# Attention and two expert stages in one kernel: undivided attention rows with their sums, keys' subtractions shared by VectorE and GpSimd, v copies on GpSimd, slots' rows scaled by GpSimd, later x stores

## The chip, the cores and the metric

The kernel runs on one core of one Trainium2 chip. The metric is the time of one execution in device microseconds. The kernel before took 1201.28 us, the median of three runs (1198.95 to 1202.61). The engines carry their names in the profile: PE is TensorE, PEld its weight loads, DVE is VectorE, ACT is ScalarE, POOL is GpSimd, SP is SyncE, which issues most DMAs.

## The reference, cut to what matters

Three stages are chained. The first is an attention without a score matrix, over 8 batches, 8 heads, 576 positions and 64 dimensions; then each of the 4608 tokens goes to the one expert of eight that its gate logits choose; then a product of two linear maps follows, with two more linear maps behind it.

```python
q_s = exp(q - max(q, axis=-1)); q_s = q_s / (sum(q_s, axis=-1) + 1e-9)
k_s = exp(k - max(k, axis=2));  k_s = k_s / (sum(k_s, axis=2) + 1e-9)
x   = einsum('bhsd,bhde->bhse', q_s, einsum('bhsd,bhse->bhde', k_s, v))   # to (4608, 512)
logits = x @ w_gate + modality_bias[modality_id]
e_idx  = argmax(logits, axis=1); gate_w = softmax(logits)[e_idx]
out[e_idx == e] = gate_w * (relu(x @ w1[e]) @ w2[e])                      # 512 -> 1024 -> 512
y = (((out @ m1) * (out @ m2)) @ w3) @ w_out
```

## The kernel before, in words

**Order of the work.** The function body() hands every step to a planner, the class Plan: a step has an engine, a guessed cost, the function that issues its instructions, and keys that it reads and writes. Plan.order() goes through the steps by readiness and priority, and the instructions are then emitted in that order; each engine runs its own in order. SP's DMAs stand in one queue, in the same way.

**Attention.** The batches are taken two at a time, in four chunks c = 0 to 3, with two sets of buffers (z = c % 2). load() brings k, q and v of a chunk, each by two DMAs of 1152 KB. keys(c) takes the maximum over positions on DVE (L304 to L307), transposes it on PE, reduces it (L316) and spreads it back to rows (L321, and ACT's copy kr, L324). Then k - kr is formed in 12 pieces of 128x384 (L330: on DVE for c = 0, on GpSimd for c = 1 to 3) and ACT takes the exponential (L331). kvs(c) copies v beside a column of ones (vp, ACT, L342), multiplies keys by values on PE (L349), divides by the keys' sums on DVE (L356 to L358, which write bd), and multiplies the result by the gate weights (L362 to L373), so that each head's 64 columns of bd are followed by one column of ones and eight columns of gate logits: 73 in all. queries(n) subtracts the row maximum of q for three of the nine token groups of a chunk (L384, L385). attend(c, j) transposes a group (PE, L399), takes the exponential (ACT, L402) and multiplies by bd (PE, L412). The 65th column of its result is the sum of a query row's exponentials, so the result must be divided by it: ACT copies the sum with 1e-9 added (L422) and the logits (L423), DVE takes the reciprocal (L424) and multiplies 512 columns by it on the way from PSUM to xt (L425). Two groups at a time are stored to x_dram (L429).

**Routing.** route(c) turns logits into the expert, the gate weight and the place of each token. early_table() and early_lists() make, from chunks 0 and 1 alone, a table of the first three slots (tab) and the lists of their tokens (ordt, written at L621 and L622), by comparing places with block numbers (L604 to L609) and one product on PE (L614).

**Slots.** A slot is up to 512 tokens of one expert. slot(P, n) loads the expert's w1 (L706) and w2, gathers the tokens' rows of x_dram by indirect DMA from POOL's queue (L715), scales each row by its gate weight (ACT, L719), transposes it (PE, L735), splits it in a high and a low part (ACT L739, DVE L740), does the same with the weights (L686 on ACT; L688 on DVE, two of eight on GpSimd) and multiplies (PE, L760, L782). All of the slots' big buffers lie where the attention's lay, so the first split waits for the last step of the attention (the key "Mb"). In the first slots GpSimd also scatters the order of all tokens (L436), and DVE and GpSimd turn the last stage's weights from 64-bit to 32-bit numbers (doubles(), L807 to L815).

**Last stage.** Products by Strassen's scheme follow (L1113, L1246). The change does not touch them.

## Time and profile before

| | |
|---|---|
| median of three runs | 1201.28 us |
| the profiled execution | 1204.72 us |
| its span | 1203.0 us |
| PE busy | 1127.9 us, 94% of the span |
| DVE busy | 855.5 us, 71% |
| ACT busy | 525.6 us, 44% |
| POOL busy | 534.8 us, 44% |
| mean granted clock of TensorE | 0.977 |

The span is that of one execution, from the first to the last instruction; the time has 1.7 us around it. The shares are averages over stages with different limits, so a stretch has to be read by itself. PE's row of the page's second part shows 3 6 7 7 7 9 9 8 in tenths over the first eight slices of 30 us, and 9 in all behind them but the last, which has 6.

### The profile page before, as it was taken

How to read it: one execution, taken by the hardware profiler on the slowest of the kernel's cores; microseconds unless marked ns; L12 is line 12 of the kernel's file. 1: busy time of each engine (PE TensorE's matmuls, PEld its weight loads, DVE VectorE, ACT ScalarE, POOL GpSimd, SP SyncE). 2: the span in 40 equal slices, each digit the busy share in tenths (PEclk: the TensorE clock that was granted, in tenths of full speed). 3: DMA queues.
4: the chain of work that ended last, by engine and by line, in shares of the span. 5: the costliest groups of instructions: out<-in, count | busy, mean ns of one | idle time of the engine just before them, and what ended most of it. 6: DMA issues, size and time to landing. Idle time of an engine off the chain costs nothing.

```text
span 1203.0 us, 22890 instructions
## 1 busy us (share of the span) xinstructions
PE 1127.9 (94%) x8605; PEld 1025.8 (85%) x8605; DVE 855.5 (71%) x1441; ACT 525.6 (44%) x1003; POOL 534.8 (44%) x538
## 2 busy tenths in 40 slices
PE   3677799899999999999999999999999999999996
PEld 3566677788788888888988999999999999999995
DVE  7989887897688887877566666657575679765550
ACT  3555465334344544533555242423232445655550
POOL 0444148663253333242241555455555576343332
PEclk9978899999999999999999999999999999999998
DMA  9982577555275467373753343434343429987741
GB/s 352 389 331 82 178 193 182 135 201 202 92 253 163 124 214 206 102 247 137 252 182 127 99 139 104 133 118 120 118 125 117 142 88 282 345 250 232 235 143 46
DMA packets 156140, 216.01 MB, mean 180 GB/s; under 512 B 19790, under 2 KB 90994, under 8 KB 156018
## 3 DMA queue, kind: packets, MB, share of 16 engines
q1 hardware_dynamic: 148946, 195.00, 50.3%
q0 software_dynamic: 7072, 19.44, 5.5%
q8 instruction: 69, 1.13, 0.4%
q14 instruction: 53, 0.43, 0.1%
HBM read 156.35 MB, written 74.82 MB: 192 GB/s over the span
## 4 chain that ended last, share of the span: by engine, by line
PE 68%; DMA 2%; DVE 0%; issue 0%; SPq 0%; ACT 0%; POOL 0%; POOLq 0%; ACTq 0%; DVEq 0%
PE pb L1113 29%; PE pb L1246 13%; PE pb L782 11%; PE pb L760 9%; PE pb L1004 4%; DMA ca<-w_f 1%; PE pb L735 1%; DMA p_dram<-ca 1%; PE pb L991 1%; DMA ca<-p_dram 0%; DVE ar L978 0%; SPq L970 0%; POOL out_dram L1220 0%; SPq L1209 0%; DVE ca L1089 0%
## 5 line engine op out<-in xcount | busy, mean ns | idle before, releaser
L1113 PE MATMUL pb<-al,ar 128*128 128x384 f32 x1728 | 308.5, 336 | 1.1 <-ACT sx L1119 0.8
L1113 PEld LDWEIGHTS pb<-al,ar 128*128 128x128 f32 x1728 | 301.1, 188 | 1.6 <-ACT sx L1119 1.1
L782 PE MATMUL pb<-ar 128*128 128x512 f32 (+1 forms) x960 | 214.0, 381 | 0.0
L760 PE MATMUL pb<-ar 128*128 128x512 f32 (+1 forms) x960 | 213.4, 383 | 0.0
L760 PEld LDWEIGHTS pb<-ar 128*128 128x128 f32 x960 | 174.7, 190 | 34.3 <-DVE ar L747 0.3
L782 PEld LDWEIGHTS pb<-ar 128*128 128x128 f32 x960 | 172.8, 188 | 32.8
L1246 PE MATMUL pb<-ar 128*128 128x256 f32 x1512 | 182.9, 283 | 2.8 <-ACT ar L977 1.6
L1246 PEld LDWEIGHTS pb<-ar 128*128 128x128 f32 x1512 | 181.8, 192 | 3.8 <-ACT ar L977 1.8
L978 DVE TENSOR_TENSOR ar<-ca,ar 128x512 fp32r<-128x512 f32 x140 | 107.8, 779 | 54.3 <-ACT ar L977 50.7
L977 ACT CAST ar<-ca 128x512 fp32r<-128x512 f32 x140 | 86.1, 622 | 45.1 <-DMA ca<-p_dram 15.0
L746 ACT ACTIVATE ar<-pb 128x512 fp32r<-128x512 f32 (+1 forms) x80 | 46.0, 577 | 116.3 <-PE pb L760 104.0
L812 POOL TENSOR_TENSOR ca<-ca 128x512 f32<-128x512 f32 x40 | 56.7, 1422 | 78.1 <-DVE ca L811 73.4
L1119 ACT COPY sx<-pb 128x384 f32<-128x384 f32 x96 | 46.0, 481 | 90.5 <-PE pb L1113 63.9
L747 DVE SCALAR_TENSOR_TENSOR ar<-pb,ar 128x512 fp32r<-128x512 f32 (+1 forms) x80 | 52.6, 659 | 39.1 <-ACT ar L746 37.9
L330 POOL TENSOR_TENSOR kt<-kt,kr 128x384 f32<-128x384 f32 x36 | 44.1, 1263 | 73.8 <-ACT kr L324 57.6
L1147 POOL TENSOR_TENSOR ca<-ca 128x384 f32<-128x384 f32 x48 | 53.5, 1115 | 49.3 <-DVE ca L1147 49.3
L785 ACT COPY yo<-pb 128x512 f32<-128x512 f32 (+1 forms) x40 | 22.6, 566 | 107.7 <-PE pb L782 94.5
L1122 POOL TENSOR_TENSOR ca<-ca,sx 128x384 f32<-128x384 f32 x24 | 27.7, 1156 | 83.2 <-ACT sx L1119 83.2
L688 DVE TENSOR_TENSOR ar<-w2r,ar 128x512 fp32r<-128x512 f32 x60 | 44.9, 775 | 27.3 <-ACT ar L686 25.2
L1119 ACT COPY ca<-pb 128x384 f32<-128x384 f32 x48 | 23.0, 481 | 87.2 <-PE pb L1113 87.2
L1113 PE MATMUL pb<-thm,ar 128*128 128x384 f32 x288 | 59.0, 340 | 0.0
L715 POOL DMA_INDIRECT ca<-x_dram,ord x38 | 38.3, 1008 | 45.5 <-DVE ord L622 20.6
(286 smaller groups left out, 1757.8 us busy)
## 6 DMA issues: line engine op xcount, KB each, us to landing
p_dram<-ca SPq DMA_DIRECT2D x168, 192.0 KB
ca<-p_dram SPq DMA_DIRECT2D x126, 256.0 KB
w1r<-in_moe_w_dram SPq DMA_DIRECT2D x10, 2048.0 KB
w2r<-in_moe_w_dram SPq DMA_DIRECT2D x10, 2048.0 KB
ca<-in_moe_w_dram SPq DMA_DIRECT2D x32, 512.0 KB
kt<-in_k_dram SPq DMA_DIRECT2D x8, 1152.0 KB
qt<-in_q_dram SPq DMA_DIRECT2D x8, 1152.0 KB
vt<-in_v_dram SPq DMA_DIRECT2D x8, 1152.0 KB
```

The source lines that it names most:

```text
L746: P.add("S", ps_(N), lambda hh=hh, p=p: SC.activation(hh(), p(), AF.Relu), r=[K("bk", pb), "Mb"], w=[K("hh", h, m) for h in hs])
L747: P.add("V", vt_(N), lambda hh=hh, hl=hl, p=p: V.scalar_tensor_tensor(out=hl(), in0=p(), scalar=0.0, in1=hh().bitcast(F32), op0=ALU.max, o ...
L760: PE.matmul(p(), lhsT=W1(i)[:, TURN[kk], ms], rhs=XT(z)[:, kk, cols], start=(kk == 0 and c == 0), stop=(kk == 3 and c == 2))
L782: PE.matmul(p(), lhsT=W2(i)[:, f, ns], rhs=HT(y)[:, f, cols], start=(f == 0 and c == 0), stop=(f == 7 and c == 2))
L812: P.add("G", gt_(512), lambda: G.tensor_tensor(Tf, Tf, Qf, op=ALU.add), r=[K("Q", b)], w=[K("T", b)])
L977: P.add("S", (ps_ if psum else sb_)(n), lambda: SC.copy(hi(), src), r=sk, w=[hk], pri=pri)
L978: P.add("V", vt_(n), lambda: V.tensor_tensor(lo(), src, hi().bitcast(F32), op=ALU.subtract), r=list(sk) + [hk], w=[lk], pri=pri)
L1004: PE.matmul(bank[pb], lhsT=th(i, quarter_of(fb, z), g, 1)[:, 0], rhs=WO(y, 4 * z + g), start=(z == 0 and g == 0 and n == 0), stop=(z == 1 ...
L1113: PE.matmul(bk(j), lhsT=Mt[:, f, a, i, m, t], rhs=X(y, x)[:, t], start=(fresh and t == 0 and n == 0), stop=(t == 1 and n == 2), skip_group ...
L1119: P.add("S", ps_(HB), lambda j=j, to=to: SC.copy(S(to), bk(j)), r=[bkk(j)], w=[sk(to)])
L1147: P.add(eng, c(HB), lambda: e.tensor_tensor(t[:, sl], x, y, op=op), r=kk, w=[k_])
L1246: PE.matmul(bk(j), lhsT=At[z][:, m, i, f], rhs=Bt[:, x, y, f], start=(fresh and f == 0 and n == 0), stop=(f == 3 and n == 2), skip_group_c ...
```

## The change

- **x rows undivided, with their sums.** attend() no longer divides. ACT copies the sum with the eight logits (72 columns) and then the 512 columns with each head's sum as a 65th (520 columns) to xt. Rows of x_dram are 520 wide (XW). The division comes later: route() adds 1e-9, takes the reciprocal and multiplies the logits; a slot does the same with its gathered rows.
- **Keys.** For c = 1 to 3 the 12 subtractions alternate between DVE and GpSimd; for c = 0 all stay on DVE.
- **v copies.** All 16 go from ACT to GpSimd.
- **Slots' rows.** In slot 0 DVE does the division and the gate weight in one instruction per tile. In the other slots DVE makes the factors (8 per row) and GpSimd multiplies 512 columns by them.
- **x stores.** Those of chunk 3 are issued after the gathers of slot 0 have landed.
- **Tables.** early_table() is written anew with fewer instructions, its constants are made at the start, and what only main_table() needs of it moves there. In early_lists() the block numbers and their products stand ahead of the comparisons of L604. The staging buffers of doubles() are named anew over the same columns.

```diff
 def keys(c):
         for g in range(4):
             hs = slice(2 * g, 2 * g + 2)
             kg = [K("k", z, g)]
-            en, e_, c_ = ("G", G, gt_(1152)) if c else ("V", V, vt_(1152))
-            for js in (slice(3 * i, 3 * i + 3) for i in range(3)):
+            for i in range(3):
+                en, e_, c_ = ("G", G, gt_(1152)) if c and "VG"[(3 * g + i) % 2] == "G" else ("V", V, vt_(1152))
+                js = slice(3 * i, 3 * i + 3)
                 P.add(en, c_ / 3 + 0.05, lambda hs=hs, e_=e_, js=js: e_.tensor_tensor(k_[:, hs, js], ..., op=ALU.subtract), r=[K("kr", z)], w=kg)
 def kvs(c):
-            P.add("S", sb_(1152), lambda g=g, w_=w_: SC.copy(w_[:, :, :, 0:64], v_[:, 2 * g : 2 * g + 2]), ...)
+            en, e_, c_ = ("G", G.tensor_copy, 1.5) if ('GGGG', 'GGGG', 'GGGG', 'GGGG')[c][g] == "G" else ("S", SC.copy, sb_(1152))
+            P.add(en, c_, lambda g=g, w_=w_, e_=e_: e_(w_[:, :, :, 0:64], v_[:, 2 * g : 2 * g + 2]), ...)
 def attend(c, j):
-        P.add("S", 0.22, lambda: SC.activation(by_bank(r_.unsqueeze(2)), pv[:, :, :, 64:65], AF.Identity, bias=eps), r=pk, w=[qk])
-        P.add("S", 0.22, lambda: SC.copy(by_bank(l_), pv[:, :, :, 65:73]), r=pk, w=[lk])
-        P.add("V", 0.2, lambda: V.reciprocal(r_, r_), w=[qk])
-        P.add("V", vt_(512), lambda: V.tensor_tensor(xdst, pv[:, :, :, 0:64], by_bank(r_.unsqueeze(2)).to_broadcast([128, 2, 4, 64]), op=ALU.mult), r=pk + [qk, lk], w=[rkey])
+        l_, lk = l2[z][:, j].rearrange("p e (b h) -> p b h e", b=2), K("l2", z, j)
+        P.add("S", 0.28, lambda: SC.copy(l_, pv[:, :, :, 64:73]), r=pk, w=[lk])
+        P.add("S", ps_(XW), lambda: SC.copy(xdst, pv[:, :, :, 0:65]), r=pk, w=[rkey])
...
+            if c == B // 2 - 1:
+                kept.append(store)
+            else:
+                store()
 def route(c, after=()):
-        vv(lambda: V.tensor_tensor(l2_, l2_, rq_.unsqueeze(3).to_broadcast([128, H, NT, E]), op=ALU.mult), ...)
+        vv(lambda: V.tensor_scalar(l2_[:, :, 0], l2_[:, :, 0], 1e-9, None, op0=ALU.add), r=list(after), w=l2k)
+        vv(lambda: V.reciprocal(l2_[:, :, 0], l2_[:, :, 0]), w=l2k)
+        vv(lambda: V.tensor_tensor(l2_[:, :, 1:], l2_[:, :, 1:], l2_[:, :, 0:1].to_broadcast([128, NT, E, H]), op=ALU.mult), ...)
 def slot(...):
-            for t, x_, xk in tiles:
-                P.add("S", sb_(512) + 0.09, lambda t=t, x_=x_: SC.activation(x_, x_, AF.Copy, scale=o[:, t, 1:2].bitcast(F32)), r=[ok], w=[xk], pri=-230)
+            for h in hs:
+                wide = xg[h].rearrange("p t (g e) -> p t g e", e=D + 1)
...
+                for group in (((0,), (1,)) if n == 0 else ((0, 1),)):
+                    P.add("V", 0.15, lambda sums=sums: V.tensor_scalar(sums, sums, 1e-9, None, op0=ALU.add), w=kk, pri=pri)
+                    P.add("V", 0.17, lambda sums=sums: V.reciprocal(sums, sums), w=kk, pri=pri)
+                for t in range(2):
...
+                    if n == 0:
+                        P.add("V", vt_(512), lambda ...: V.scalar_tensor_tensor(out=to, in0=rows[:, :, 0:D], scalar=gate, in1=rows[:, :, D : D + 1].to_broadcast([128, H, D]), op0=ALU.mult, op1=ALU.mult), ...)
+                        continue
+                    P.add("V", 0.15, lambda ...: V.tensor_scalar(rows[:, :, D], rows[:, :, D], gate, None, op0=ALU.mult), ...)
+                    P.add("G", gt_(512), lambda ...: G.tensor_tensor(to, rows[:, :, 0:D], rows[:, :, D : D + 1].to_broadcast([128, H, D]), op=ALU.mult), ...)
 ...
     slot(P, 0)
+    for store in kept:
+        store([K("arrived", K("xg", h, t)) for h in range(2) for t in range(2)])
```

The first place is DVE between the division by the keys' sums of chunk 3 (bd) and the token lists (ord). In the kernel before the lists are written among the divisions of chunk 3's groups (ca<-pp is L425, the write of xt):

```order
L385 TENSOR_TENSOR qs_134<-qt_130,qx_132 128x8x3x64
L620 TENSOR_REDUCE qt_129<-pb_75 128x12
L425 TENSOR_TENSOR ca<-pp_83,ca 128x512
L621 CAST ord<-qt_129 128x12
L424 RECIPROCAL ca<-ca 128x8
L622 TENSOR_REDUCE ord<-pb_75 128x12
L425 TENSOR_TENSOR ca<-pp_82,ca 128x512
```

Now nothing of the attends stands on DVE; behind bd come the six comparisons (L623), the last of the queries (L386), the lists (L634 to L636), and at once slot 0's gathered rows (L740 to L746):

```order
L359 TENSOR_TENSOR bd_153<-pb_76,rk_149 128x4x64
L623 TENSOR_TENSOR qt_128<-qt_128 128x384 x6
L386 TENSOR_TENSOR qs_133<-qt_129,qx_131 128x8x3x64
L634 TENSOR_REDUCE qt_128<-pb_75 128x12
L635 CAST ord<-qt_128 128x12
L636 TENSOR_REDUCE ord<-pb_75 128x12
L740 TENSOR_SCALAR ca<-ca 128x8
L741 RECIPROCAL ca<-ca 128x8
L746 SCALAR_TENSOR_TENSOR ca<-ca,ord 128x512
```

Nine pairs of L424 and L425 that followed bd are gone from DVE, and the lists stand nearer to bd.

The second place is POOL from chunk 2's subtractions (kt0) to the first weights of slot 0. Before:

```order
L330 TENSOR_TENSOR kt0_116<-kt0_116,kr0_143 128x2x192 x12
L330 TENSOR_TENSOR kt1_117<-kt1_117,kr1_144 128x2x192 x12
L587 IOTA qt0_129 128x128
L715 DMA ca_95<-x_dram_59,ord_94 128x512 x4
L688 TENSOR_TENSOR ar_2303<-w1r_1386,ar_2303 128x512 x2
```

Now, from the same IOTA on (chunk 3's subtractions are kt1, its v copies vp):

```order
L603 IOTA qt0_128 128x128
L330 TENSOR_TENSOR kt1_116<-kt1_116,kr1_143 128x2x192 x5
L343 COPY vp0_138<-vt1_118 128x18x64
L330 TENSOR_TENSOR kt1_116<-kt1_116,kr1_143 128x2x192
L343 COPY vp1_139<-vt1_118 128x18x64
L732 DMA ca_94<-x_dram_59,ord_93 128x520 x6
L705 TENSOR_TENSOR ar_2224<-w1r_1395,ar_2224 128x512
```

Twelve subtractions of a chunk became six, four v copies joined them, and two gathers of slot 1 stand directly behind slot 0's four.

The third place is SP's queue at the first expert weights. Before, the stores of chunk 3 (L429) follow w1, and w2 stands behind the last of them:

```order
L671 TENSOR_LOAD tab_158 x8
L706 ISA
L706 DMA w1r_1386<-in_moe_w1_dram 128x4x1024
L429 DMA x_dram_59<-ca_95 128x1024
L793 ISA
L793 DMA order2_64<-ord_94 128x4x2
```

Now w2 follows w1, and the five stores of chunk 3 (L428) come behind both:

```order
L723 DMA w1r_1395<-in_moe_w1_dram 128x4x1024
L723 ISA
L723 DMA w2r_1396<-in_moe_w2_dram 128x8x512
L428 DMA x_dram_59<-ca_94 128x1040 x4
L428 DMA x_dram_59<-ca_94 128x520
L824 ISA
```

The wait of w2 for slot 0's gathers now stands ahead of the stores.

## Rows read from the trace of the kernel before

**Rows 1.** Windows by stage: length, busy us of each engine, PE's clock, DMA share, GB/s

```profile
20.00:83.00 63.00, 44.60 (x1184) 36.75 (x1188) 56.05 (x97) 34.91 (x68) 22.09 (x18) 0.90 1.04 386
83.00:153.00 70.00, 55.23 (x1534) 46.10 (x1529) 62.70 (x154) 38.91 (x96) 26.19 (x24) 0.82 0.42 137
153.00:258.00 105.00, 97.63 (x449) 78.93 (x450) 86.51 (x197) 51.07 (x94) 72.17 (x96) 0.97 0.59 150
258.00:1203.00 945.00, 927.15 (x5428) 861.85 (x5427) 638.59 (x968) 397.36 (x745) 411.77 (x385) 0.99 0.53 169
```

**Rows 2.** Groups by form, 0 to 153 us: busy us, mean ns, idle before

```profile
L330 POOL TENSOR_TENSOR kt<-kt,kr 128x384 f32<-128x384 f32 x36 | 44.1, 1263 | 73.8 <-ACT kr L324 57.6 <-DVE qx L384 16.2
...
L425 DVE TENSOR_TENSOR ca<-pp,ca 128x512 f32<-128x512 f32 x36 | 24.5, 687 | 1.6 <-DVE ca L424 0.2 <-issue 0.2 <-PE pb L399 0.2
...
L402 ACT ACTIVATE qT<-pb 128x512 f32<-128x512 f32 x36 | 21.1, 606 | 10.0 <-PE pb L399 8.8 <-remote 1.2
...
L342 ACT COPY vp<-vt 128x1152 f32<-128x1152 f32 x16 | 18.1, 1161 | 9.0 <-PE pb L349 4.6 <-DMA vt<-in_v_dram 3.2 <-issue 1.3
...
L422 ACT ACTIVATE ca<-pp,eps 128x8 f32<-128x8 f32 x36 | 9.9, 275 | 21.7 <-PE pp L412 16.8 <-remote 3.2 <-DVE mx L306 1.3
L423 ACT COPY ca<-pp 128x64 f32<-128x64 f32 x36 | 7.4, 207 | 0.0
L424 DVE RECIPROCAL ca<-ca 128x8 f32<-128x8 f32 x36 | 6.7, 192 | 7.1 <-ACT ca L422 3.7 <-issue 3.3
...
L330 DVE TENSOR_TENSOR kt<-kt,kr 128x384 f32<-128x384 f32 x12 | 5.7, 552 | 0.0
...
L604 DVE TENSOR_TENSOR qt<-qt 128x384 bf16<-128x384 f32 x6 | 2.9, 553 | 0.0
...
L609 DVE TENSOR_TENSOR qt<-qt 128x1080 bf16<-128x1080 f32 x1 | 2.1, 2094 | 0.0
...
L262 POOL MEMSET zer<- 128x584 int32 x1 | 0.6, 612 | 0.0
```

**Rows 3.** Timeline, DVE, 44 to 60 us: start, us, instruction

```profile
50.26 0.68 DVE L425 TENSOR_TENSOR ca<-pp,ca 128x512 f32<-128x512 f32 x1
50.86 0.19 DVE L424 RECIPROCAL ca<-ca 128x8 f32<-128x8 f32 x1
50.97 1.30 DVE L304 TENSOR_TENSOR tr<-kt 128x1024 f32<-128x1024 f32 x1
```

**Rows 4.** Line L385: min, median, max ns; first and last start

```profile
L385 DVE TENSOR_TENSOR qs<-qt,qx x12: 1709/1753/2395, 22.8 to 139.2; 128x1536 f32<-128x1536 f32 x12
```

**Rows 5.** Timeline, 65 to 90 us: a wait of DVE; two attends on PE

```profile
67.03 0.16 DVE L356 TENSOR_SCALAR rk<-pb 128x4 f32<-128x4 f32 x1 [4.44 <-PE pb L349]
...
72.54 1.25 PE L412 MATMUL pp<-bd,qT 64*64 64x73 f32 x64
```

**Rows 6.** Timeline from chunk 3's bd to slot 0's first product

```profile
130.06 0.42 DVE L358 TENSOR_TENSOR bd<-pb,rk 128x256 f32<-128x256 f32 x1
...
132.90 0.19 ACT L373 COPY bd<-pb 128x32 f32<-128x32 f32 x1 [0.92 <-PE pb L370]
...
135.15 1.11 PE L399 MATMUL pb<-ident,qs 128*128 128x128 f32 x4
...
136.19 2.30 PE L412 MATMUL pp<-bd,qT 64*64 64x73 f32 x64
...
141.71 0.16 DVE L622 TENSOR_REDUCE ord<-pb 128x12 f32<-128x36 f32 x1
...
145.63 0.27 ACT L422 ACTIVATE ca<-pp,eps 128x8 f32<-128x8 f32 x1 [3.22 <-remote]
...
152.60 0.69 DVE L425 TENSOR_TENSOR ca<-pp,ca 128x512 f32<-128x512 f32 x1 [0.20 <-DVE ca L424]
...
154.60 0.72 ACT L719 ACTIVATE ca<-ca,ord 128x512 f32<-128x512 f32 x1 [0.38 <-DMA ca<-x_dram,ord]
...
157.34 23.02 PE L760 MATMUL pb<-ar 128*128 128x512 f32 x96
```

More of the change, by code (lines that the diff above doesn't have):

```diff
@@ L62, in add @@
         deps.discard(i)
[L63 removed]
+        self.steps.append((eng, cost, fn, sorted(deps), i + pri + self.shift, slack))
     def order(self):
@@ L254, in setup @@
         V.tensor_scalar(cnt, iota8, float(NTOK), None, op0=ALU.mult)
+        table_setup()
         for t in oh_:
             V.memset(t[:, NT], 0.0)
-        V.memset(eps, 1e-9)
         for t in vp:
@@ L443, in route @@
         z = c % 2
-        l2_, rq_, l, m, el, eq, oh, s, pos, pf = (t[z] for t in (l2, rq, lg, mm_, el_, eq_, oh_, s_, pos_, pf_))
-        l2k, rqk = [[K(x, z, t) for t in range(NT)] for x in ("l2", "rq")]
+        l2_, l, m, el, eq, oh, s, pos, pf = (t[z] for t in (l2, lg, mm_, el_, eq_, oh_, s_, pos_, pf_))
+        l2k = [K("l2", z, t) for t in range(NT)]
         bc = lambda t: t.unsqueeze(2).to_broadcast([128, NT, E])
@@ L484, in body @@
     row = lambda n, shape=(128, E), d=F32: const.tile(list(shape), d, name="t_" + n)
-    base, base_i, left, early, gone, late = row("base"), row("basei", d=I32), row("left"), row("early"), row("gone", (128, 1)), row("late", (128, 1))
+    base, left, early, gone, late = row("base"), row("left"), row("early"), row("gone", (128, 1)), row("late", (128, 1))
     seen = [row(f"seen{i}", (128, n)) for i, n in enumerate((NE, ND, NF + NX))]
@@ L540, in count @@
         return ji, j
-    def doubles_table(nm, col, ns, n, b0, first, sc, w):
-        s = floors(nm, n, 0, 9)
-        a = running(nm, s)
-        ji, j = count(nm, ns)
-        vv(lambda: V.tensor_copy(j, ji))
-        lookup(nm, col, ns, j, s, a, b0, 2 * TS, sc, w=w)
-        d = row(nm + "d", (128, ns))
-        vv(lambda: V.tensor_scalar(d, j, float(2 * TS), first, op0=ALU.mult, op1=ALU.add))
-        vv(lambda: V.scalar_tensor_tensor(out=d, in0=j, scalar=a[:, 7:8], in1=d, op0=ALU.is_lt, op1=ALU.mult))
-        vv(lambda: V.tensor_scalar(tab[:, 2, col : col + ns], d, float(JUNK), None, op0=ALU.add), w=w)
-        return a
+    f8, upto = row("f8"), row("upto", (128, E, E))
@@ L560, in early_table @@
-        c = taken("ta", a, NE, early)
-        vv(lambda: V.tensor_scalar(gone, c[:, 7:8], float(2 * TS), -float(JUNK), op0=ALU.mult, op1=ALU.add))
+        vv(lambda: V.tensor_scalar(w, left, 1.0 / (2 * TS), -0.499, op0=ALU.mult, op1=ALU.add))
+        vv(lambda: V.tensor_scalar(s, w, big, -big, op0=ALU.add, op1=ALU.add))
+        vv(lambda: V.tensor_tensor(prod, upto, s.unsqueeze(1).to_broadcast([128, E, E]), op=ALU.mult), w=[K("eq", 0)])
+        vv(lambda: V.tensor_reduce(filled, prod, axis=AX.X, op=ALU.add), r=[K("eq", 0)])
@@ L625, in main_table @@
         b0, b1, mid, held = row("b0"), row("b1"), row("mid"), row("held")
+        vv(lambda: V.memset(early, 0.0), r=[K("opened")])
+        c = taken("ta", filled, NE, early)
+        vv(lambda: V.tensor_scalar(gone, c[:, 7:8], float(2 * TS), -float(JUNK), op0=ALU.mult, op1=ALU.add))
         vv(lambda: V.tensor_tensor(left, cnt, base, op=ALU.subtract), r=[K("cnt")])
```

88 lines of the change are left out of this document (54 added, 34 removed).

## The prediction, as it went on record

> **What bounds the kernel now.** I read the page's shares first, then windows by stage, then the groups of the first 153 us, then the timeline where the stages meet. The windows [rows 1] show three regimes. From 258 us on PE is busy 927 of 945 us at a clock of 0.99: what the change does to DVE, ACT or POOL there costs or brings nothing unless it makes PE wait. From 153 to 258 us PE is busy 97.6 of 105. Before 153 us no engine holds PE's place: from 20 to 83 us the DMA engines are full (share 1.04) and bring q, k and v; from 83 to 153 us they are not (0.42), and DVE is busy 62.7 of 70 us, PE 55.2 at a mean clock of 0.82. The border at 83 us is where the share falls. From there on the attention is held by DVE, with PE close behind. The change is worth the time by which slot 0's first product, at 157.34 us [rows 6], comes earlier. All behind it moves along as one block.
>
> I set a mark at chunk 3's bd (the second of its two writes begins at 130.06 and ends at 130.48 us [rows 6]). Up to it DVE's queue decides; from it to 157.34 us, 26.9 us, two chains run side by side: the nine attends of chunk 3, and the lists, gathers and transposes of slot 0.
>
> **The change, up to the mark.** (1) Removed from DVE: 36 reciprocals and 36 divisions [rows 2], of which 27 pairs stand ahead of the mark. Their durations overlap; by starts a division takes 0.60 us (50.26 to 50.86) and a reciprocal 0.11 (50.86 to 50.97) [rows 3]. 27 x 0.71 = 19.2 us less.
> (2) Added to DVE: half of 36 subtractions. DVE's own twelve of chunk 0 took 5.7 us, 0.476 each [rows 2]; 18 x 0.476 = 8.6 us more.
> (3) What these 18 cost more because GpSimd works beside them is not in the trace. Bounds: none at all, or each waits for a whole GpSimd piece, 1.26 us [rows 2], which is 22.7 us. The nearest row is L385, also with two inputs in SBUF: 1.75 us in the median and 2.40 at worst [rows 4], so up to 0.64 more beside GpSimd's pieces. I take half of that, 0.3 each: 5.4 us. What POOL's other work costs DVE today stays about as it is: 18 subtractions of 1.26 us leave POOL (22.7 us), and 16 v copies come.
> (4) A v copy on GpSimd has no row. Its 1152 columns at the memset's pace (612 ns for 584 columns) take 1.2 us, at the subtraction's (1263 ns for 384, two inputs) 3.8 [rows 2]. I take 1.6, nearer to the memset, as the copy, too, reads less than the subtraction. A chunk then costs POOL 6 x 1.26 + 4 x 1.6 = 14.0 us where its subtractions cost 15.2, so POOL's queue is no longer than before; at 3.8 it is 22.8, and two chunks' worth of that, 46 us, still fits the 70 in which POOL is busy 26 today [rows 1]. ACT loses 18.1 us of copies and the 17.3 of L422 and L423, and takes 36 copies of 520 columns, each about the 0.61 of L402, and 36 small ones of 0.21 [rows 2], 29.5 us in all: 6 us less, with work that was DVE's.
> (5) The early table and lists lose some 17 small instructions at 0.11 to 0.2 us, about 3 us; but the block products (L609, 2.1 us [rows 2]) and a dozen small ones now stand ahead of the mark, 3.5 us more. Route's extra reciprocal and addition are within the rounding.
> (6) A stall goes: DVE waited 4.44 us for chunk 1's products [rows 5], whose keys came piece by piece from GpSimd. Six pieces take half of twelve, so I take off 4. What is late next there is the landing of chunk 2's keys, behind full DMA engines.
> The sum to the mark: -19.2 + 8.6 + 5.4 - 3 + 3.5 - 4 = -8.7 us; the mark falls at 121.8.
>
> **From the mark on.** The attends' chain took 22.8 us to the end of the last division (153.29) and 4.05 more to the first product. On DVE it loses nine pairs. It contains one stall of 3.22 us in which ACT waits for no engine of this core [rows 6]; I don't count on its going. PE decides how much the pairs are worth: two attends' products take 1.25 us in one place [rows 5] and 2.30 in this stretch [rows 6]: 2.4 and 1.2 GHz, the two levels whose mean here is 0.82 [rows 1]. With its transposes (1.11 us [rows 6]) an attend takes PE about 2.2 us at the lower level, so nine take 20, and 10 at the upper one. The gates are in bd 2.6 us after the mark (133.09 [rows 6]), so the chain is 23 us at the low level and 13 at the high one, and 27 or 17 to the first product. I take 23, nearer to the low level, whose rows stand in this stretch.
> The gathers' chain: the lists were ready 11.4 us behind the mark (141.87), the last gathered tile was there 12.7 us later (154.6), and the first product began 2.8 us after that [rows 6]. The lists now stand directly behind six comparisons (2.9 us [rows 2]) and one q subtraction (1.75), with the small ones some 5.5 us behind the mark. The stores of chunk 3 are no longer among the gathers, so 12.7 is the upper end and I take 11; the division on DVE stands in for ACT's scaling. 5.5 + 11 + 1 + 2.8 = 20.3 us, under the other chain. So from the mark to the first product 23 instead of 26.9 us: -3.9.
> **The slots.** Each later slot has four GpSimd instructions of 512 columns more, and ACT four fewer. POOL is busy 72 of 105 us in the first slots [rows 1], where the scatters stand; four pieces for each of two slots, 1.7 us each at L330's pace for 512 columns, are 13.5 of the 33 left. The cover is PE's own work on the slot before, 23.0 us for the first half of slot 0 [rows 6]. If it fails, PE waits at a transpose. I take 0, with 3 us to either side. The deferred stores are read first by slot 3's gathers, with three slots of such work ahead of it.
> **Sum.** -8.7 - 3.9 = -12.6, taken as -13: the profiled execution, 1204.7 us (span 1203.0), would take 1191.7. It stands 3.4 us above the median 1201.3, so the median would be 1188.3; I say 1188.
>
> **The rivals.** *A, GpSimd and DVE take turns.* In the place of the division DVE waits at each subtraction for GpSimd's piece: 22.7 us instead of 5.4, and the mark is at +8.6 instead of -8.7. With the attends' -3.9, and some 3 us because v copies meet the q subtractions as well, the first product comes 8 us later: 1209. It decides from about 1.0 us lost per subtraction (0.3 and 12.6/18). For it: the slowest L385 [rows 4]. Against: its twelve instructions reach over all of GpSimd's rounds, and none lost more than 0.64. The Trainium skill's page "SBUF — State Buffer", section "SBUF: two separate sides", says that a VectorE operation with two SBUF inputs and a GpSimd operation that reads SBUF exclude each other for a whole instruction. By that rule each of the 18 would wait up to a whole piece, as in A; the 0.64 agrees with a wait but not with a whole piece each time.
> *B, the tail is the bound.* PE works 55.2 of the 70 us at a low clock [rows 1]; if it stays there, DVE's relief turns into waits for PE, and only the 4 us of the stall [rows 5] are won: 1197.5, as the first product is then due 27 us after the last attends could begin, as before. For it: PE's share. Against: DVE has only 7 us of idle time in the 70, so it, not PE, is the one that others wait for.
> *C, DVE stops being a bound at all.* Nothing is lost to GpSimd (-5.4), PE runs at the high level with less waiting (-5): 1178. For it: the DMA engines are done at 83 us [rows 1], 47 us ahead of the mark. Against: DVE's work up to there does not shrink by as much as the mark would move.
>
> **How the numbers follow.** The forecast has 0.57, C 0.17, B 0.15, A 0.11. The forecast's own range is 1181 to 1195 (5.4 us of contention up or down, 3 of the slots). The range to C and B that leaves out at most 2 in 10 is 1177 to 1199. About 0.3%, 3.6 us, is what a measurement of this kernel tells from no change; faster than that are the forecast, C and a third of B: 0.77; within it the rest of B and a little of A: 0.12; slower 0.11.
>
> **What would show it.** L425's heirs stand on ACT at about 0.6 us, and the groups of L330 on DVE show 0.5 to 0.9 us, not 1.5 and more (A). The mark (the last bd of chunk 3) lies near 122 us, the first product of slot 0 near 145. DVE's wait for chunk 1's products is under 1 us. PE is busy 98% from 245 us on, with no new wait of a transpose for POOL. The prediction is wrong if the mark moves and the first product does not (B), or if the first product moves and PE loses it again between 150 and 300 us.

## The result and the profile after

| | median of 5 runs | lowest to highest | profiled execution (span) |
|---|---|---|---|
| before | 1201.28 us | 1198.95 to 1202.61 | 1204.72 (1203.0) |
| after | 1207.39 us | 1206.53 to 1211.26 | 1207.34 (1205.6) |

The change makes the kernel slower: the ratio is 1.006 [1.0041, 1.0079], 6.1 us where 13 us less were forecast. 1207.4 lies outside the range of 1177 to 1199.

The stages of the kernel after, in the columns of [rows 1]:

```profile
20.00:83.00 63.00, 44.23 (x1084) 38.10 (x1088) 52.25 (x82) 25.71 (x49) 19.23 (x15) 0.76 1.00 363
83.00:153.00 70.00, 51.91 (x1584) 44.86 (x1580) 59.82 (x116) 41.07 (x90) 28.55 (x23) 0.87 0.44 165
153.00:258.00 105.00, 98.68 (x505) 80.45 (x498) 92.30 (x219) 46.83 (x88) 80.40 (x103) 0.94 0.54 138
258.00:1205.00 947.00, 928.01 (x5437) 861.83 (x5435) 668.63 (x1023) 383.51 (x722) 444.66 (x411) 1.00 0.53 170
```

DVE lost 27 reciprocals and 27 divisions ahead of the mark, and yet it is not freed there: what it does up to the mark, the end of chunk 3's bd, takes as long as before, and it waits longer. First before, then after, from the start to the mark:

```profile
0.00:130.48 130.48, 85.00 (x2370) 70.49 (x2370) 114.35 (x229) 67.90 (x136) 46.88 (x54) 0.91 0.74 276
```

```profile
0.00:134.49 134.49, 86.80 (x2355) 74.72 (x2355) 115.36 (x205) 59.67 (x118) 47.72 (x50) 0.84 0.73 267
```

DVE (third figure behind the length) ran 24 instructions fewer and was busy 1.0 us longer; its idle time is 16.1 before (130.48 - 114.35) and 19.1 after. What grew most is its wait for the keys' products, 20 us to the mark, before and after (in all, times, longest):

```profile
DVE rk L356 <- PE pb L349: 5.0, 2, 4.4
```

```profile
DVE rk L357 <- PE pb L350: 8.8, 2, 5.1
```

From the mark on I cut the span at the first product of slot 0 and at the last write of the fourth slot's output. All times of this table are of the two profiled executions:

| us | before | after | difference | forecast |
|---|---|---|---|---|
| DVE busy up to the mark | 114.35 | 115.36 | +1.0 | -4.7 |
| DVE idle up to the mark | 16.13 | 19.13 | +3.0 | -4 |
| mark to first product | 26.9 | 25.8 | -1.1 | -3.9 |
| first product to the end of the fourth slot | 193.9 | 197.0 | +3.1 | 0 |
| the rest of the span | 851.7 | 848.3 | -3.4 | 0 |
| sum | 1203.0 | 1205.6 | +2.6 | -12.6 |

Without the last difference the sum is +6.0; the medians differ by 6.1. The profiled execution of before stood 3.4 us above its own median, so I take most of that row for its own scatter: in the traces of the experiments below (without f3) this rest is 848.2 to 848.9 us in eleven and 850.5 to 851.9 in six, and e2 and f5, whose programs are the same there, lie on different sides. But some 1.4 us of it is no scatter. In 300 us of the last stage, with PE busy throughout, before and f2 (before with the sharing alone) ran 1723 matmuls, and after, f1 and h4 ran 1731. Before, then after:

```profile
700.00:1000.00 300.00, 300.00 (x1723) 300.00 (x1722) 200.24 (x286) 102.68 (x193) 172.25 (x145) 1.00 0.42 124
```

```profile
706.00:1006.00 300.00, 300.00 (x1731) 300.00 (x1730) 202.78 (x290) 104.81 (x198) 172.98 (x146) 1.00 0.43 125
```

The prediction put what the change does there at nothing unless PE has to wait; no run shows why PE is 0.5% faster.

Three groups of the kernel after, 0 to 153 us, beside [rows 2]:

```profile
L330 DVE TENSOR_TENSOR kt<-kt,kr 128x384 f32<-128x384 f32 x30 | 25.5, 904 | 0.3 <-ACT kr L323 0.3
...
L330 POOL TENSOR_TENSOR kt<-kt,kr 128x384 f32<-128x384 f32 x18 | 22.8, 1297 | 25.3 <-ACT kr L323 22.0 <-PE pp L415 3.3
L343 POOL COPY vp<-vt 128x1152 f32<-128x1152 f32 x16 | 22.4, 1409 | 47.1 <-DMA vt<-in_v_dram 25.9 <-PE pb L350 11.2 <-issue 9.9
```

DVE's 30 subtractions took 25.5 us where 12 took 5.7. One correction to the part on the change: the order suggested that w2 waits for slot 0's gathers and the stores of chunk 3 for both. On the chip there was no such wait. w2 was issued at 138.77 us, ahead of the first gather at 139.56, and three of the five stores at 140.18, 143.37 and 145.52 us, while the gathered rows came at 147.5 to 150.8. So w2 and these stores stood beside the gathers.

### The profile page after: what moved, and what is told of

It is laid out like the page before. It is cut to its first block, busy times and chain, and to the rows that moved or that the text cites. A ratio compares the mean times of both kernels' runs of the same rounds, so it can differ in the third digit from the quotient of the medians.

```text
span 1205.6 us, 22929 instructions
## 1 busy us (share of the span) xinstructions
PE 1126.1 (93%) x8605; PEld 1027.4 (85%) x8605; DVE 885.1 (73%) x1467; ACT 499.0 (41%) x949; POOL 576.8 (48%) x568
## 4 chain that ended last, share of the span: by engine, by line
PE 69%; DVE 1%; DMA 1%; issue 0%; ACT 0%; POOL 0%; SPq 0%; POOLq 0%; DVEq 0%; ACTq 0%
PE pb L1146 29%; PE pb L1279 13%; PE pb L813 12%; PE pb L791 10%; PE pb L1037 4%; PE pb L766 1%; PE pb L1024 1%; DVE ar L1011 1%; DMA ca<-p_dram 0%; DMA p_dram<-ca 0%; POOL out_dram L1253 0%; SPq L1242 0%; DVE ca L1122 0%; ACT ar L1010 0%; DVE ca L1167 0%
## 5 line engine op out<-in xcount | busy, mean ns | idle before, releaser
L1180 POOL TENSOR_TENSOR ca<-ca 128x384 f32<-128x384 f32 x48 | 53.4, 1112 | 45.4 <-DVE ca L1180 45.3
L705 DVE TENSOR_TENSOR ar<-w2r,ar 128x512 fp32r<-128x512 f32 x60 | 50.1, 874 | 10.4 <-ACT ar L703 9.6
L732 POOL DMA_INDIRECT ca<-x_dram,ord x38 | 39.7, 1044 | 36.8 <-PE pb L766 14.8
L705 POOL TENSOR_TENSOR ar<-w1r,ar 128x512 fp32r<-128x512 f32 x20 | 27.9, 1393 | 58.2 <-ACT ar L703 49.0
## 6 DMA issues: line engine op xcount, KB each, us to landing
w1r<-in_moe_w_dram SPq DMA_DIRECT2D x10, 2048.0 KB, 10.7
w2r<-in_moe_w_dram SPq DMA_DIRECT2D x10, 2048.0 KB, 11.7
qt<-in_q_dram SPq DMA_DIRECT2D x8, 1152.0 KB, 11.7
```

The costliest lines, as they stand in the source:

```text
L705: P.add(g, c, lambda: e.tensor_tensor(lo(), raw(), hi().bitcast(F32), op=ALU.subtract), r=[K(nm + "r", i), K(nm + "h", i), extra], w=[K(nm ...
L1180: P.add(eng, c(HB), lambda: e.tensor_tensor(t[:, sl], x, y, op=op), r=kk, w=[k_])
```

## The experiments

Every kernel was timed against the kernel before on the same chip; ratios are to that run, with the 95% interval. The other columns are from each kernel's trace: the mark, slot 0's first product, and from there to the end of the fourth slot. Kernels of one letter were timed together; all others, after among them, are compared by their ratios only.

| kernel | mark | first product | four slots | ratio |
|---|---|---|---|---|
| before | 130.5 | 157.3 | 193.9 | 1 |
| after | 134.5 | 160.3 | 197.0 | 1.0060 [1.0041, 1.0079] |
| e1: v copies on ACT | 132.9 | 157.1 | 203.1 | 1.0052 [1.0032, 1.0072] |
| e2: keys on DVE | 131.9 | 155.3 | 199.7 | 1.0042 [1.0019, 1.0065] |
| e3: maxima whole | 134.3 | 157.8 | 205.5 | 1.0072 [1.0045, 1.0100] |
| e4: gathers late | 134.1 | 157.2 | 204.6 | 1.0065 [1.0043, 1.0087] |
| f1: rows only, keys on GpSimd | 137.5 | 160.2 | 201.3 | 1.0067 [1.0043, 1.0092] |
| f2: sharing only | 155.4 | 185.3 | 193.2 | 1.0190 [1.0161, 1.0218] |
| f3: scaling on ACT | 135.4 | 160.9 | 221.7 | 1.0284 [1.0256, 1.0312] |
| f5: e1 + e2 | 129.4 | 155.5 | 200.7 | 1.0026 [1.0008, 1.0044] |
| g1: f5 + maxima | 131.0 | 154.7 | 204.4 | 1.0070 [1.0043, 1.0097] |
| g2: g1 + gathers late | 130.5 | 155.1 | 207.7 | 1.0075 [1.0049, 1.0101] |
| g3: f5 + scaling on DVE | 128.9 | 153.5 | 202.1 | 0.9990 [0.9969, 1.0011] |
| g4: g2 + scaling on DVE | 132.3 | 156.8 | 193.1 | 0.9954 [0.9933, 0.9975] |
| h1: scaling on DVE | 135.4 | 160.7 | 198.4 | 1.0014 [0.9994, 1.0034] |
| h4: maxima, gathers, scaling | 135.4 | 159.1 | 190.4 | 0.9949 [0.9927, 0.9971] |
| h5: g4 + w2 late | 134.3 | 157.7 | 195.2 | 0.9963 [0.9939, 0.9987] |
| h6: w2 late | 136.2 | 163.1 | 202.6 | 1.0052 [1.0030, 1.0075] |
| i1: scaling, gathers | 134.3 | 156.0 | 196.3 | 0.9999 [0.9986, 1.0012] |
| i2: scaling, maxima | 135.3 | 158.2 | 201.5 | 1.0052 [1.0034, 1.0070] |

**The sharing of the keys and v copies.** e1 puts the v copies back on ACT and e2 all subtractions on DVE, both in the order in which the planner had put them; f5 does both.

```diff
-            ... lambda g=g, w_=w_, e_=e_: e_(w_[:, :, :, 0:64], ...)     # e1
+            ... lambda g=g, w_=w_: SC.copy(w_[:, :, :, 0:64], ...)
-                ... lambda hs=hs, e_=e_, js=js: e_.tensor_tensor(...)     # e2
+                ... lambda hs=hs, e_=V, js=js: e_.tensor_tensor(...)
```

> The changed kernel, with the 16 v copies given back to ScalarE; every engine's order is otherwise kept as it was planned. Contention theory (DVE's work grew because GpSimd works beside it): chunk 0's twelve subtractions take 5.7 us again instead of 7.6, L306 and L292 beside the copies 0.45 instead of 1.4, chunk 1's products no longer wait for copies, chunk 3's bd (at 134.5 us after the change) ends 3 to 5 us earlier, and the time is 1203 to 1205 us. Order theory (other steps were put into two chains that set the end): the place of chunk 1's key rows (kr at 54.1 us) hardly moves, bd of chunk 3 at most 2 us, and the time is 1205 to 1208 us.

> The changed kernel, with all twelve key subtractions of every chunk on DVE and none on GpSimd; every engine's order is otherwise kept. Contention theory: the 18 shared pieces took DVE 17.9 us (0.99 each), so 36 undisturbed ones at 0.48 take 17.1: DVE loses nothing, a chunk's subtractions are done in 6 instead of 8 to 9 us, and the time falls by 2 to 4 us, to 1203 to 1205. Rival (the sharing did relieve DVE): DVE has 8.6 us more to do ahead of the mark, which ends 5 to 8 us later, and the time is 1212 to 1216 us.

> The changed kernel, with nothing left for GpSimd in the attention: all subtractions on DVE, all v copies on ScalarE; the orders are otherwise kept as planned. Contention theory: with each part alone bd of chunk 3 ended 1.6 and 2.6 us earlier than after the change (134.5), so with both it ends at 129.5 to 131 us, and the first product of slot 0 starts at 152 to 155 us instead of 160.3. If all behind it moves along, the time is 5 to 8 us below the changed kernel, about that of the kernel before. Slots theory: the first four slots take longer by what the first product gains (200 us and more), they still end at 353 us or later, and the ratio to the kernel before stays at 1.003 or above.

By themselves e1 and e2 bring the mark 1.6 and 2.6 us earlier (3 to 5 were expected of e1), and in e1 chunk 0's twelve subtractions take 5.70 us again. Their ratios can't be told from after's.

f5's group of the subtractions, 0 to 140 us, and its window to the mark:

```profile
L330 DVE TENSOR_TENSOR kt<-kt,kr 128x384 f32<-128x384 f32 x48 | 23.3, 551 | 0.5 <-ACT kr L323 0.5
```

```profile
0.00:129.40 129.40, 84.93 (x2354) 72.95 (x2354) 103.67 (x223) 75.39 (x133) 2.63 (x16) 0.87 0.75 277
```

Without GpSimd 48 subtractions take 23.3 us on DVE; with it 30 take 25.5. So giving 18 of them away cost DVE time. But although DVE was busy 10.7 us less than before (103.67 for 114.35), the mark came only 1.1 us earlier. Against after, whose order it keeps, DVE is busy 11.7 us less, the mark comes 5.1 us and the first product 4.7 us earlier, but the fourth slot ends only 1.0 us earlier. The ratio falls by 0.0034, at intervals that just overlap. The waits of f5's DVE, 20 to 130 us:

```profile
DVE rk L357 <- PE pb L350: 11.0, 2, 6.0
DVE ca L452 <- ACT ca L423: 3.7, 1, 3.7
```

The first was 5.0 us before, and the second isn't there before: together they are the 9.6 us by which f5's DVE is idle longer (25.7 for 16.1). PE is not full meanwhile. For the same products it waits for ACT's exponentials, and these wait for DVE's subtractions:

```profile
PE pb L350 <- ACT kt L331: 15.7, 5, 5.1
```

```profile
ACT kt L331 <- DVE kt L330: 10.4, 5, 4.2
```

f5 is above before all the same, and its first four slots took 6.8 us longer than before's.

**One part of the change alone.** f1 keeps the undivided rows and takes the sharing away (all keys of chunks 1 to 3 on GpSimd, copies on ACT, planned anew); f2 is the kernel before with the sharing alone, planned anew too.

```diff
-                en, e_, c_ = ... if c and "VG"[(3 * g + i) % 2] == "G" else ...
+                en, e_, c_ = ... if c and "GG"[(3 * g + i) % 2] == "G" else ...
-            en, e_, c_ = ... if ('GGGG', 'GGGG', 'GGGG', 'GGGG')[c][g] == "G" else ...
+            en, e_, c_ = ... if ('SSSS', 'SSSS', 'SSSS', 'SSSS')[c][g] == "G" else ...
```

> The changed kernel, with the keys' subtractions of chunks 1 to 3 all on GpSimd and the v copies on ScalarE, as before the change, and planned anew: what is left is the undivided rows, the slots' scaling, the tables and the later stores. If sharing with GpSimd is what cost the time, DVE has lost 19 us of divisions here and gained nothing, chunk 3's bd ends at 122 us or earlier and the time is at least 4 us under that of the kernel before. Rival: a chunk's keys come out of GpSimd in 12 pieces over 15 us, and this chain, not DVE's work, sets when each chunk can go on; then bd of chunk 3 ends at 127 to 132 us, DVE waits for products by some 10 us more, and the time is that of the kernel before to 4 us above it.

> The kernel before with the other part alone: the keys' subtractions alternate between DVE and GpSimd, the v copies are on GpSimd; the divisions stay in the attends. Contention theory: 18 pieces of 1.0 us and lengthened neighbours come on top of a DVE that was full, bd of chunk 3 ends at 138 to 146 us instead of 130.5, and the time is 8 to 14 us above the kernel before. Rival (the shorter chain of keys repays it): bd at 130 to 134 us, and the time within 4 us of the kernel before.

f1's window to the mark, then f2's:

```profile
0.00:137.50 137.50, 87.64 (x2360) 75.36 (x2361) 108.70 (x193) 76.11 (x135) 52.67 (x52) 0.83 0.70 261
```

```profile
0.00:155.40 155.40, 92.77 (x2370) 79.94 (x2370) 126.63 (x244) 52.21 (x120) 46.35 (x52) 0.80 0.63 232
```

In f1 DVE is busy 5.7 us less than before (the lists' six comparisons, 5.4 us, now stand ahead of its mark) and idle 12.7 more (28.8 for 16.1): the mark falls 7 us later, and the relief is gone. f2 shows what the sharing costs where the divisions stay: DVE is busy 12.3 us more, idle 12.6 more. Its slots are not changed and take as long as before's, 193.2 us: the end of the fourth is 27.3 us later than before's in the two profiled executions, where the ratio of the medians gives 23 (0.019 x 1204). Both marks lie outside what either theory expected.

**The maxima and the gathers.** In the kernel after the planner put three query steps of 1.75 us among the maxima of chunk 1's keys. e3 hands the four maxima to the planner as one step; e4 moves slot 0's gathers behind the last attends by their slack.

```diff
-            P.add("V", vt_(1024), ...)      # e3: and three more
+            P.add("V", vt_(1024) + vt_(512) + 2 * vt_(256), maxima, ...)
-                ... slack=1.0 if n == 0 else 4.0)     # e4
+                ... slack=7.0 if n == 0 else 4.0)
```

> The changed kernel, with the four maxima of half a chunk's keys planned as one step, so that no query step is put between them. Order theory: chunk 1's key rows (kr) come at 45 to 47 instead of 54.1 us, its bd at 68 instead of 76, chunk 3's loads of k start 6 to 8 us earlier, the mark (bd of chunk 3, 134.5 us) ends 4 to 7 us earlier and the time is 1200 to 1203 us. Contention theory: DVE is busy without a gap from 77 us on, its work is the same, and only part of the 5.1 us in which it waited for chunk 1's products goes: the mark moves by under 3 us and the time stays at 1205 or more.

> The changed kernel, with one number of the planner changed (slot 0's gathers are taken to land 6 us later), so that TensorE does the last attends of chunk 3 before it waits for slot 0's gathered rows. Order theory: the waits of 3.9 and 1.6 us go, the last attend's copy ends at about 151 instead of 157.2 us, slot 0's first product starts at 155 to 156 instead of 160.3, and the time is 1202 to 1204 us. Rival (the DMA engines, full with both expert weights, hold the gathered rows back): the rows come no earlier than now, at 147.5 to 151.7, so the transposes end at 153 at the earliest, the splits wait for weights as well, and the first product is at 158 or later: 1205 or more.

Chunk 1's key rows on ACT, before, after and in e3:

```profile
44.08 0.59 ACT L324 COPY kr<-pb 128x512 f32<-128x512 f32 x1 [1.78 <-PE pb L321]
```

```profile
54.13 0.59 ACT L323 COPY kr<-pb 128x512 f32<-128x512 f32 x1 [0.37 <-PE pb L320]
```

```profile
45.40 0.59 ACT L327 COPY kr<-pb 128x512 f32<-128x512 f32 x1 [0.37 <-PE pb L324]
```

e3's window to the mark:

```profile
0.00:134.30 134.30, 83.32 (x2382) 71.62 (x2382) 120.30 (x210) 60.59 (x120) 49.05 (x50) 0.87 0.73 269
```

e3 brought the rows 8.7 us forward and DVE's idle time fell to 14.0 us; but DVE was busy 4.9 us longer (120.30), 3.1 of them in the subtractions (28.6 for 25.5), and the mark stayed. e4 brought the first product forward, 157.2 for 160.3; then PE lost it at a branch of the program (L939), where it waited 7.74 us for DVE's queue (in after it lost 1.7 there):

```profile
335.39 1.94 PE L766 MATMUL pb<-ident,ca 128*128 128x128 f32 x8 [7.74 <-DVEq L939]
```

**The scaling of the slots' rows.** f3 lets ACT scale the rows of the later slots, in eight activations per tile, with the planner's order kept. h1 lets DVE do it as in slot 0.

```diff
-                    P.add("G", gt_(512), ... G.tensor_tensor(to, rows[:, :, 0:D], ...))     # f3
+                    P.add("G", gt_(512), ... [SC.activation(to[:, e], rows[:, e, 0:D], AF.Copy, scale=rows[:, e, D : D + 1]) for e in range(H)])
-                    if n == 0:     # h1
+                    if n < 100:
```

> The changed kernel, with the scaling of slots 1 and later by ScalarE (eight activations of 64 columns a tile) instead of GpSimd; every order is otherwise kept as planned. Slots theory (the first four slots are bound by DVE and GpSimd, whose instructions there lengthen each other; they take 196.9 us after the change and took 193.8 before): POOL loses 2 us per pair of tiles, the waits of TensorE for transposes of slots 1 to 3 shrink, the four slots take 193 to 195 us and the time falls by 2 to 4 us against the changed kernel (ratio to before 1.003 to 1.004). Rival (the four slots wait for DVE's own longer list of steps, the table and the last weights' conversion, at the branch behind them): they take 196 to 198 us and the time does not change (ratio 1.005 to 1.007).

> The changed kernel with one thing changed: the rows of all slots are scaled by DVE in one instruction a tile instead of by GpSimd. Slots theory: without sharing in the attention the same step gave 0.0036 of the ratio (1.0026 to 0.999); alone it should give as much, 4 us: ratio 1.001 to 1.004, and GpSimd's last scatter some 4 us earlier than 252.6. Rival (it helped only because the first product was earlier there): ratio 1.005 to 1.007.

The scaling of four slots, 155 to 350 us: after, f3 and h1:

```profile
L750 POOL TENSOR_TENSOR ca<-ca 128x512 f32<-128x512 f32 x16 | 18.7, 1196 | 8.3 <-DVE ca L748 8.3
```

```profile
L752 ACT ACTIVATE ca<-ca 128x64 f32<-128x64 f32 x128 | 44.2, 348 | 13.9 <-DVE ca L748 10.3
```

```profile
L746 DVE SCALAR_TENSOR_TENSOR ca<-ca,ord 128x512 f32<-128x512 f32 x16 | 12.7, 831 | 0.0
```

f3 says nothing of GpSimd: 128 small activations took 44.2 us on ACT, and PE waited 4.3 us for them directly (160 to 362 us) and 14.8 for DVE's splits, each of which follows a step on ACT. h1 is clearly faster than after (the intervals lie apart), by 0.0046 or 5.5 us, although its first product came at 160.7. Its four slots of one execution, 198.4, don't show it; its scatters end 4.8 us earlier on POOL (the last starts at 247.78 for 252.55).

**Both kinds together.** g1 is f5 with e3's maxima, g2 that with e4's gathers, g3 is f5 with h1's scaling, g4 all of them. h4 is g4 with the sharing as in after.

> Nothing of the attention on GpSimd (subtractions on DVE, copies on ScalarE) and the maxima of half a chunk as one step, in the order planned for the shared kernel. Account by DVE's busy and idle time up to chunk 3's bd: without sharing it was busy 103.7 us (and idle 25.7), with the maxima whole it was idle 14.0 (and busy 120.3 with sharing). If both hold together, bd ends at 118 to 121 us and the first product starts at 141 to 146 instead of 160.3. If all behind moves along, the ratio to the kernel before is 0.990 to 0.994. Slots theory (GpSimd's queue of scatters, gathers, splits and scalings, which ended at 250 to 254 us however early the first product began, sets the end of the first four slots): they take 206 us and more, end at 352 to 357, and the ratio is 0.999 to 1.003.

> The same, with slot 0's gathers planned to land 6 us later, so that the last attends stand ahead of the transposes. The first product starts 2 to 4 us earlier than without this. Slots theory: the time does not change by it (within 2 us). If the slots move along: 2 to 4 us less.

> Nothing of the attention on GpSimd (ratio 1.0026 by itself, first four slots 200.7 us), and the rows of all slots are scaled by DVE in one instruction a tile, as slot 0's are, instead of by GpSimd. Slots theory: GpSimd has 17 us less to do in the first four slots, its last scatter starts at 245 us or earlier instead of 250.9, the four slots take 195 to 198 us, and the ratio is 0.998 to 1.001. Rival (DVE is the fuller engine there, busy 96 of 105 us): DVE gets 0.75 us a tile more and gives back only the factors and the contention, the four slots take 200 us or more, and the ratio stays at 1.002 to 1.005.

> All together: no sharing in the attention, maxima whole, late transposes, DVE scaling in all slots. If the attention's 15 us and the slots' relief add up: first product at 140 to 144 us, first four slots 197 to 203 us, ratio 0.986 to 0.993. If the slots hold the end whatever comes before: ratio 0.996 to 1.000.

> The best kernel so far (nothing of the attention on GpSimd, maxima whole, late transposes, DVE scaling: ratio 0.9954), with the sharing put back: subtractions alternating, v copies on GpSimd, same order. Contention theory: DVE is busy some 15 us longer up to chunk 3's bd, which ends 3 us or more later than 132.3, the first product starts 2 to 5 us later than 156.8, and the ratio is 0.998 to 1.001. Rival (in this order DVE has room for it, since it waits for others for 25 us there anyway): ratio 0.994 to 0.997.

g1 refutes a mark at 118 to 121: it stood at 131.0. In its window DVE is busy 107.4 us and waits 11.8 us in five places for the products (L361), and PE waits ahead of these products 12.3 us in three places for ACT (5.4 for a v copy, 4.2 for an attend's copy, 2.7 for an exponential). g2's first product comes no earlier than g1's, and g4's at 156.8, not at 140 to 144.

After, f5, h1 and g3 are the change with both of its GpSimd parts, without the sharing, without the scaling and without either: 1.0060, 1.0026, 1.0014 and 0.9990. g3 and g4 have the same scaling and lie 0.0036 apart at overlapping intervals. h4 and g4 differ in the sharing alone: 0.9949 and 0.9954, no difference in this order. Both are faster than before and than after (h4's median 1200.06, that of before on its chip 1206.53).

**What is left of them.** i1 and i2 take the maxima or the gathers out of h4. h5 and h6 put the stores of chunk 3 ahead of w2 in SP's queue, in g4 and in after.

```diff
-    for store in kept:
-        store(...)            # moved into slot 0, ahead of w2 (h5, h6)
```

> The changed kernel with DVE scaling in all slots and slot 0's gathers planned 6 us later; sharing and the maxima as in the change. If the last attends behind the transposes cost what TensorE waited there (3.9 and 1.6 us): first product at 155 to 158 instead of 160.3 us, the first four slots 191 to 195 us, ratio 0.995 to 0.998. Rival (the slots still eat an earlier first product): ratio 1.000 to 1.003.

> The changed kernel with DVE scaling in all slots and the maxima of half a chunk as one step; transposes as in the change. If the maxima were worth nothing in the attention (bd of chunk 3 at 134.3 instead of 134.5 us with them): first product at 157 to 161 us and ratio 1.000 to 1.003. Rival: the keys' earlier chain pays at the lists and gathers, first product at 156 us or earlier, ratio 0.995 to 0.998.

> The best kernel so far, with w2 of slot 0 issued behind the stores of chunk 3, as in the kernel before. If w2's 2 MB hold the gathered rows back, the rows land 2 to 4 us earlier, the first product starts 1 to 3 us earlier than 156.8, and the ratio is 0.992 to 0.995. Rival (the rows are paced by GpSimd's issue and by the attends in front, or w2 is then late for its splits): ratio 0.995 to 0.998.

> The changed kernel, with only w2 of slot 0 issued behind the stores of chunk 3. If w2 holds the rows back, DVE's wait of 8.1 us for the first of them falls to 4 to 6, TensorE's waits of 3.9 and 1.6 us for transposed rows fall to 2 us together, the first product starts at 156 to 158 instead of 160.3, and the ratio is 1.003 to 1.005. Rival: no change at the rows (147.5), ratio 1.005 to 1.008.

w2's place is no cause: h5 is at g4 and h6 at after within the intervals. The five pairs that differ in the scaling alone all have one sign: after to h1 -0.0046, f5 to g3 -0.0036, e3 to i2 -0.0020, e4 to i1 -0.0066, g2 to g4 -0.0121. The intervals lie apart in the first and the last two of them, and only g2 and g4 were timed together. The maxima have not: +0.0012 (after to e3), +0.0044 (f5 to g1), +0.0038 (h1 to i2), -0.0050 (i1 to h4). Nor have the gathers: +0.0005 (after to e4), +0.0005 (g1 to g2), -0.0015 (h1 to i1), -0.0103 (i2 to h4). What these two are worth stays open: each of them has the planner write the slots anew.

## Why the prediction was wrong

**"From there on the attention is held by DVE."** This is the step that failed. DVE being busy 62.7 of 70 us made it look like the bound. The runs took up to 10.7 us of work from it (f5 against before), and the mark came 1.1 us earlier; in one and the same order (f5 against after) it was 5.1 for 11.7. The keys' chain, which goes from DVE's subtractions over ACT's exponentials to PE's products and back to DVE, runs close under it: of f5's 25.7 us of idle time on DVE (129.40 - 103.67), 11.0 are waits for the keys' products (5.0 before) and 3.7 a wait for an attend's copy on ACT. How much of these waits is the planner's order, which was made for other costs, no run separates. Rival B's sentence, that DVE's relief turns into waits for PE, is what f5, f1 and g1 show, though B's time (1197.5) counted on the stall going, and its reason, that PE is the bound, is not shown: up to the mark PE is busy 84.9 us in f5 and 85.0 before, and waits for ACT. g3, the undivided rows with neither the sharing nor GpSimd's scaling, is at 0.9990 [0.9969, 1.0011]: taking the divisions off DVE and putting the keys' 36 subtractions in their place is worth nothing that can be measured. The change then costs what its GpSimd parts cost, in the order that it has.

**Terms 1 to 3, the sum on DVE.** The divisions went. The 18 subtractions cost 17.9 us (25.5 of the group less 7.6 of chunk 0's twelve), 0.99 each, not 8.6 + 5.4: the 0.3 of contention was 0.52. DVE's timeline of the kernel after has the twelve of chunk 0 and five beside GpSimd, POOL's the six pieces that ran at that time:

```profile
17.18 7.60 DVE L330 TENSOR_TENSOR kt<-kt,kr 128x384 f32<-128x384 f32 x12
...
55.96 6.29 DVE L330 TENSOR_TENSOR kt<-kt,kr 128x384 f32<-128x384 f32 x5
```

```profile
54.81 7.02 POOL L330 TENSOR_TENSOR kt<-kt,kr 128x384 f32<-128x384 f32 x6 [12.99 <-ACT kr L323]
```

These five took 1.26 each, 0.78 more than the 0.476 without GpSimd. Rival A's price was 1.26 more, and A was to decide from about 1.0; over all 18 the mean, 0.52 more, lies between the forecast and A. And chunk 0's twelve, which stayed on DVE, took 7.6 us instead of 5.7, since the v copies stand beside them (5.70 in e1, without the copies). These are +3.9 and +1.9, as much as the 5.7 us by which DVE's busy time missed the forecast. DVE saved nothing by the sharing: f5 was busy 103.67 us with 36 subtractions of chunks 1 to 3; without half of them, at 23.3/48 = 0.485 each, it would be 94.9, so that 20.4 us of after's 115.36 come from GpSimd's work beside it. In the kernel before it was some 9.5 us, by an estimate with the forecast's own prices: f5 has 1.2 us less work than before (-19.2 + 17.5 - 3 + 3.5) and was busy 10.7 us less. So the change added 11 us of it where 5.4 were allowed. A's time, 1209, was the nearest of all, but its mechanism is not the cause by itself: without the sharing f5 is still slower than before, and h4, which has it, is as fast as g4, which has not.

**Term 4, the v copy.** 1.41 us in the mean, near the 1.6 of the forecast. That was right, and so was POOL's queue: 47.7 us busy up to the mark, 46.9 before.

**Term 6, the stall that goes.** It grew. The forecast took its cause to be GpSimd's pieces, and half of the pieces to end nearly all of it (4 of 4.44). It was 5.08 us, and DVE waited another 3.73 for chunk 0's products (0.6 before). In the kernel after the keys' rows came 10 us later, as the planner had set query steps among the maxima:

```profile
42.04 1.21 DVE L303 TENSOR_TENSOR tr<-kt 128x1024 f32<-128x1024 f32 x1
43.17 1.75 DVE L386 TENSOR_TENSOR qs<-qt,qx 128x1536 f32<-128x1536 f32 x1
44.84 0.68 DVE L304 TENSOR_TENSOR tr<-tr 128x512 f32<-128x512 f32 x1
45.45 1.74 DVE L385 TENSOR_REDUCE qx<-qt 128x24 f32<-128x1536 f32 x1
47.11 0.41 DVE L305 TENSOR_TENSOR mx<-tr 128x256 f32<-128x256 f32 x1
47.44 1.75 DVE L386 TENSOR_TENSOR qs<-qt,qx 128x1536 f32<-128x1536 f32 x1
...
75.56 0.23 DVE L357 TENSOR_SCALAR rk<-pb 128x4 f32<-128x4 f32 x2 [5.08 <-PE pb L350]
```

It was in the order of the instructions, and I did not follow DVE's row there. But e3 shows that the row's order alone is worth nothing here: with the rows back at 45.4 DVE was idle 5.1 us less and busy 4.9 us longer.

**From the mark on.** "Under the other chain" failed for the gathers. The lists were ready 4.9 us behind the mark (5.5 forecast) and the last tile was there at 150.8, 11.4 us later (11). That 11 came out is partly luck: it counted on the stores being gone from among the gathers, and three of them and w2 stood there. But 3.8 us from there to the first product became 9.5, since PE's queue has three attends between the transposes; in e4, which moves them, the first product comes 3.0 us earlier. PE's timeline of after:

```profile
148.75 0.48 PE L766 MATMUL pb<-ident,ca 128*128 128x128 f32 x1 [3.89 <-DVE ca L746]
150.85 0.90 PE L766 MATMUL pb<-ident,ca 128*128 128x128 f32 x3 [1.62 <-DVE ca L746]
151.68 2.23 PE L415 MATMUL pp<-bd,qT 64*64 64x73 f32 x64
153.84 1.10 PE L402 MATMUL pb<-ident,qs 128*128 128x128 f32 x4
155.69 0.74 PE L415 MATMUL pp<-bd,qT 64*64 64x73 f32 x32 [0.75 <-ACT qT L405]
156.36 0.65 PE L766 MATMUL pb<-ident,ca 128*128 128x128 f32 x4
158.48 1.97 PE L766 MATMUL pb<-ident,ca 128*128 128x128 f32 x8 [1.46 <-DVE ar L771]
160.27 24.47 PE L791 MATMUL pb<-ar 128*128 128x512 f32 x96
```

**"All behind it moves along as one block."** False for the first four slots. f5's first product came 4.7 us before after's, in the same order, and its fourth slot ended 1.0 us before. e2's first product came 2 us before that of before, and e2 is slower; h4's came 1.8 us later, and h4 is faster. From the fifth to the eighth slot the kernels take 45.4 us per slot (only f3's fifth took 51.4); the first four take 190 to 222. PE from 160 to 350 us, before, after and h4:

```profile
160.00:350.00 190.00, 183.02 (x843) 150.07 (x842) 150.28 (x294) 86.29 (x156) 106.53 (x124) 0.99 0.57 172
```

```profile
160.00:350.00 190.00, 181.39 (x827) 148.40 (x826) 163.98 (x333) 75.64 (x136) 121.97 (x137) 0.98 0.51 147
```

```profile
160.00:350.00 190.00, 186.71 (x857) 152.77 (x858) 165.26 (x341) 78.02 (x140) 108.86 (x123) 0.99 0.56 157
```

POOL has 15.4 us more in them after the change and PE runs 16 matmuls fewer. "The slots 0 +- 3" was the other mis-sized term: GpSimd's scaling costs some 5 us (after to h1, by the ratios). How it does that the traces show in places only. One is where GpSimd's piece of L705 holds up DVE's small step (L740) towards the factors, and with it GpSimd's own scaling (L750):

```profile
283.64 1.29 POOL L705 TENSOR_TENSOR ar<-w1r,ar 128x512 fp32r<-128x512 f32 x1 [4.06 <-ACT ar L703]
285.61 4.75 POOL L750 TENSOR_TENSOR ca<-ca 128x512 f32<-128x512 f32 x4 [0.68 <-DVE ca L748]
```

```profile
283.70 1.28 DVE L740 TENSOR_SCALAR ca<-ca 128x16 f32<-128x16 f32 x1
...
285.58 0.18 DVE L740 TENSOR_SCALAR ca<-ca 128x16 f32<-128x16 f32 x1
```

Of the 17 such steps of L740 one other was as long, 1.69 us, and it too ended with GpSimd's L705 (at 173.8); the rest took 0.17 to 0.31. With h4's edits the four slots take 190.4 us; which part is the scaling and which the order that the planner writes with it, no run separates.
